# A linear-attention and token-mixer kernel: the attention output transposed by DMA instead of on TensorE, stores on SP, and one explicit table of steps

## The chip, the cores and the metric

The kernel runs on 1 core of a Trainium2 chip. The metric is the device time of one execution in microseconds. Engines are named as in the profile: PE is TensorE's matmul, PEld its weight load, DVE VectorE, ACT ScalarE, POOL GpSimd, SP SyncE. SPq and ACTq are the queues of SP and ACT when they issue DMAs. L12 is line 12 of the kernel before.

## The reference

Four batches, eight heads, 768 time steps, head size 48: a recurrent linear attention with a decay for each channel, followed by a token mixer.

```python
# attention; r, k, v, w: [4, 8, 768, 48]; u: [8, 48]
for t in range(S):
    cur = einsum('bhd,bhe->bhde', u[None] * kt, vt)
    y[:, :, t] = einsum('bhd,bhde->bhe', rt, state + cur)
    state = wt[:, :, :, None] * state + einsum('bhd,bhe->bhde', kt, vt)
# mixer; x = y as [4, 768, 384]; d_hyper = 64
wq, wk = x @ w_q, x @ w_k
W_tok = einsum('bsd,btd->bst', wq, wk) / sqrt(d_hyper)
out = maximum(einsum('bst,btd->bsd', W_tok, x), 0) @ w_out
```

## The kernel before

The 768 steps of a batch are cut into three tiles of 256 steps, so there are 12 tiles n = 3b + m. In a tile, partition p holds steps 2p and 2p + 1 (index j), and the partitions 0 to 63 and 64 to 127 are two chunks of 128 steps (index q). The state goes from chunk to chunk.

A tile runs through named steps, each a small Python function that issues its instructions:

- `load` (L146): w, k, r, v, 384 KB each, from SP, into buffers three deep.
- `log` (L153, ACT), `sums` (L158, PE): logarithm of the decay and its running sums, as matmuls with triangular matrices, into three PSUM tiles `cw`. `expk`, `expr`, `decay` (ACT) exponentiate them.
- `kdec` (L205, POOL) and `rdec` (L196, DVE): k and r times the decays, `KdS` and `RdS`. `uk1`, `uk2` (POOL), `red` (DVE), `vd` (POOL): the diagonal term, from `u*k*r`. `vcast` (ACT) writes v as bf16.
- `trR` (L214, PE), `evT` (L224, DVE): both decayed operands transposed into the PSUM tile `psT`, 16 transposes, and copied to `RKT`.
- `amat` (L230, PE), `mask` (L240, DVE): the products A inside a chunk, for each j, and their masking.
- `state`, `stadd` (PE), `stev` (L298, DVE): the new state in PSUM tile `Sn`, written to `SB`.
- `ymat` (L308), `yst` (L319), `yd` (L330), all PE: the output Y of the tile from A, from the state and from the diagonal.
- `yev` (L338): Y to bf16 as `X`. `xtr` (L348): X transposed on PE, six 128 x 128 blocks, into the PSUM tile `xt_ps`. `xev` (L358): copied to `XT`. `qkmat` (L365, PE) and `qkev` (L380): the products with w_k and w_q.

A batch then runs `tmat` (L386), `tev`, `mix` (L402), `mixev`, `fin` (L416), `finev` (L424), `store` (L431): since the mixer has no softmax, it is computed as a 64 x 384 matrix `Tps`, then `mps`, a ReLU and the product `fps` with w_out. A pair of output chunks goes out with two DMAs of 192 KB.

PSUM holds two large buffers (`psT`, A, `Sn`, Y take turns, L114) and four small ones (`cw`, `xt_ps`, `qk`, `Tps`, `mps`, `fps`, L117). An allocation waits until the use before it in that slot is done.

Seven tuples at L45 to L51 say which engine makes a copy: `EX` for X, `ET` for XT, `EQ` for qk, `EM` for the ReLU, `EF` for the output, 1 for ACT and 0 for DVE; `ES` says for each store whether ACT or SP issues it.

Every engine works in the order in which its instructions are issued. Before the change, each step has a due time (L501 to L665): a list of offsets for a first, a middle and a last tile, added to a start time for each tile, and the same for batches; the steps are sorted by due time (L681). `u` is loaded by `uload`, and `ucast` spreads it over the partitions with two f32 matmuls into `ups` and a DVE copy to `ubc`.

Of the kernel before, what the change touches and what calls it, by code (L numbers as in the profile page):

```python
# [12 lines left out]
BF16 = mybir.dt.bfloat16  # L13
# [12 lines left out]
def kernel(  # L26
# [12 lines left out]
    nc = tc.nc  # L39
# [5 lines left out]
    EX = (1, 1, 1, 1, 1, 1, 1, 1, 1, 1, 1, 0)  # L45
    ET = (1, 1, 1, 1, 0, 0, 0, 0, 0, 1, 1, 0)
    EQ = (1, 0, 1, 0, 0, 0, 1, 0, 1, 1, 1, 0)
    EM = (1, 1, 1, 0, 1, 0, 0, 1, 1, 0, 1, 1, 1, 1, 1, 1, 1, 1, 1, 0, 1, 1, 0, 1)
    EF = (0, 1, 0, 1, 1, 1, 1, 0, 0, 1, 1, 0, 1, 1, 1, 1, 1, 1, 0, 0, 0, 0, 0, 0)

    ES = (1, 0, 0, 1, 0, 1, 1, 1, 1, 1, 1, 0, 1, 1, 1, 1, 1, 1, 0, 1, 0, 1, 0, 0)  # L51
# [57 lines left out]
    sm = ctx.enter_context(tc.tile_pool(name="sm", bufs=3))  # L109
# [22 lines left out]
    plan = []  # L132

    def at(t, fn):
        plan.append((t, len(plan), fn))

    T = {}
# [6 lines left out]
    def load(n, nm, ap):  # L146
        b, m = divmod(n, NU)
        src = ap[b, :, ds(m * C2, C2)]
        t = ld.tile([C, H, D2], F32, name=nm + "G", tag=nm + "G")
        nc.sync.dma_start(out=t, in_=src.rearrange("h (p j) d -> p h (j d)", j=2))  # L150
        T[nm, n] = t
# [62 lines left out]
    def trR(n, j):  # L214
        T["trR", n, j] = True
        if ("psT", n) not in T:
            T["psT", n] = big([C, 2, 2, NP, C], BF16, "psT")
        o = T["psT", n][:, j]
        src = T[("Rd", "Kd")[j], n]
        for hp in range(NP):  # L220
            for jj in range(2):
                mm(o[:, :, hp, ds(jj * HC, HC)], src[:, jj, hp], ID128, trans=True)

    def evT(n):  # L224
        need(("trR", n, 0), ("trR", n, 1))
        RKT = bt.tile([C, 2, 2, NP, C], BF16, name="RKT", tag="RKT")
        nc.vector.tensor_copy(RKT, T["psT", n])  # L227
        T["RKT", n] = RKT

    def amat(n, js):  # L230
        RKT = T["RKT", n]
        A = big([C, 2, NP, C], F32, "A")
        for hp in range(NP):
            for q, hh in ((0, 0), (1, 1), (1, 0), (0, 1)):
                mm(A[ds(q * HC, HC), hh, hp],
                   RKT[ds(hh * 64, D), 1, q, hp, ds(js * HC, HC)],
                   RKT[ds(hh * 64, D), 0, q, hp], start=(hp == 0))
        T["A", n, js] = A
# [80 lines left out]
    def yst(n):  # L319
        T["yst", n] = True  # L320
        b, m = divmod(n, NU)
        for q in range(2):
            if 2 * m + q:
                SB = T["SB", b, 2 * m + q]
                for hp in range(NP):
                    mm(T["Y", n][:, q, ds(hp * D2, D2)], T["RKT", n][:, 0, q, hp],
                       SB[:, ds(hp * D2, D2)], start=False)
# [10 lines left out]
    def yev(n):  # L338
# [3 lines left out]
        if m == 0:  # L342
            T["X", b] = xpool.tile([C, NCH, DM], BF16, name="X", tag="X")
            T["XT", b] = xpool.tile([128, NK, S], BF16, name="XT", tag="XT")
# [3 lines left out]
    def xtr(n):  # L348
        need(("yev", n))
        b, m = divmod(n, NU)  # L350
        tp = mtile([128, NK, C2], BF16, "xt_ps")
        for cc in range(2):
            for dt in range(NK):
                mm(tp[:, dt, ds(cc * C, C)],
# [3 lines left out]
    def xev(n):  # L358
        T["xev", n] = True
        b, m = divmod(n, NU)  # L360
        copy(ET[n], T["XT", b][:, :, ds(m * C2, C2)], T["tp", n])
# [3 lines left out]
    def qkmat(n):  # L365
# [4 lines left out]
        for cc in range(2):  # L370
            for kt in range(NK):
                mm(qk[:, cc], XT[:, kt, ds((2 * m + cc) * C, C)], wk_sb[:, kt],
                   start=(cc == 0 and kt == 0))
        for kt in range(NK):
            for q in range(2):
                mm(qk[ds(q * DH, DH), 2:4].rearrange("p c h -> p (c h)"), T["wq"][:, kt],
                   XT[:, kt, ds((2 * m + q) * C, C)], start=False)
# [46 lines left out]
    def finev(b, c):  # L424
        T["finev", b, c] = True
        if c % 2 == 0:
# [66 lines left out]
    def wcast():  # L493
# [7 lines left out]
    steps = [  # L501
        (-3.67, log, ()),
        (-1.33, uk1, ()),
        (-0.45, sums, ()),
        (-0.42, expk, ()),
        (-0.25, expr, ()),
        (1.36, kdec, ()),
        (1.89, rdec, ()),
        (2.24, decay, ()),
        (3.56, uk2, ()),  # L510
        (5.7, trR, (1, )),
        (5.95, trR, (0, )),
        (5.99, vcast, ()),
        (6.48, red, ()),
        (6.51, vd, ()),
        (7.46, evT, ()),
        (8.59, amat, (0, )),
        (9.91, amat, (1, )),
        (10.1, mask, (0, )),
        (10.73, mask, (1, )),  # L520
        (11.87, state, ()),
        (11.9, stadd, (0, )),
        (12.36, stev, (0, )),
        (13.55, stadd, (1, )),
        (14.38, stev, (1, )),
        (15.25, ymat, ()),
        (15.48, yst, ()),
        (15.48, yd, ()),
        (15.51, yev, ()),
        (17.44, xtr, ()),  # L530
        (18.18, xev, ()),
        (20.45, qkmat, ()),
        (20.75, qkev, ()),
    ]
    first = [
        (-6.23, log, ()),
        (-6.05, sums, ()),
        (-2.68, expk, ()),
        (-0.31, decay, ()),
        (0.59, uk1, ()),  # L540
        (1.7, expr, ()),
        (3.15, kdec, ()),
        (5.93, trR, (1, )),
        (6.95, rdec, ()),
        (6.98, trR, (0, )),
        (7.64, evT, ()),
        (8.73, uk2, ()),
        (9.1, red, ()),
        (9.65, amat, (0, )),
        (9.93, amat, (1, )),  # L550
        (11.0, mask, (0, )),
        (12.22, mask, (1, )),
        (13.97, vcast, ()),
        (14.21, state, ()),
        (14.64, stadd, (0, )),
        (15.85, ymat, ()),
        (16.28, stev, (0, )),
        (16.31, stadd, (1, )),
        (16.31, yst, ()),
        (16.86, stev, (1, )),  # L560
        (16.87, vd, ()),
        (16.9, yd, ()),
        (17.07, yev, ()),
        (18.09, xtr, ()),
        (18.76, xev, ()),
        (20.43, qkmat, ()),
        (20.46, qkev, ()),
    ]
    last = [
        (-8.43, log, ()),  # L570
        (-0.36, sums, ()),
        (-0.33, expk, ()),
        (0.3, expr, ()),
        (0.33, rdec, ()),
        (0.47, decay, ()),
        (1.66, kdec, ()),
        (5.38, vcast, ()),
        (6.06, uk1, ()),
        (6.69, trR, (0, )),
        (7.03, trR, (1, )),  # L580
        (7.36, evT, ()),
        (7.73, uk2, ()),
        (9.43, amat, (0, )),
        (10.04, amat, (1, )),
        (11.58, state, ()),
        (13.51, red, ()),
        (14.13, mask, (0, )),
        (15.69, stadd, (0, )),
        (15.84, vd, ()),
        (15.86, mask, (1, )),  # L590
        (16.87, stev, (0, )),
        (17.84, ymat, ()),
        (17.87, yst, ()),
        (17.87, yd, ()),
        (21.51, stadd, (1, )),
        (29.8, yev, ()),
        (29.83, xtr, ()),
        (33.23, xev, ()),
        (33.26, qkmat, ()),
        (33.29, qkev, ()),  # L600
        (35.83, stev, (1, )),
    ]
    bsteps = [
        (-0.2, tmat, (0, )),
        (-0.17, tmat, (1, )),
        (0.03, tmat, (2, )),
        (0.67, tev, ()),
        (1.72, mix, (0, )),
        (1.75, mixev, (0, 0, )),
        (1.75, mixev, (0, 1, )),  # L610
        (3.02, mix, (1, )),
        (3.05, mixev, (1, 0, )),
        (3.05, mixev, (1, 1, )),
        (5.18, mix, (2, )),
        (5.5, mixev, (2, 0, )),
        (6.82, mixev, (2, 1, )),
        (7.09, fin, (0, )),
        (8.59, fin, (1, )),
        (8.71, fin, (2, )),
        (9.55, finev, (0, )),  # L620
        (9.58, finev, (1, )),
        (12.6, finev, (2, )),
        (13.11, store, (0, )),
        (13.4, fin, (3, )),
        (13.43, finev, (3, )),
        (15.19, store, (1, )),
        (15.4, fin, (4, )),
        (16.51, fin, (5, )),
        (16.54, finev, (4, )),
        (19.42, finev, (5, )),  # L630
        (19.68, store, (2, )),
    ]
    blast = [
        (12.66, tmat, (0, )),
        (12.96, tmat, (1, )),
        (13.44, tmat, (2, )),
        (13.55, tev, ()),
        (13.58, mix, (0, )),
        (14.09, mix, (1, )),
        (14.09, mix, (2, )),  # L640
        (14.12, mixev, (0, 0, )),
        (14.12, mixev, (0, 1, )),
        (14.12, mixev, (1, 0, )),
        (14.12, mixev, (2, 0, )),
        (14.63, mixev, (1, 1, )),
        (28.34, mixev, (2, 1, )),
        (28.37, fin, (0, )),
        (28.5, fin, (1, )),
        (29.14, fin, (2, )),
        (29.18, fin, (3, )),  # L650
        (29.23, finev, (0, )),
        (29.26, finev, (1, )),
        (29.73, store, (0, )),
        (29.74, fin, (4, )),
        (30.7, finev, (2, )),
        (31.09, finev, (3, )),
        (31.34, fin, (5, )),
        (33.84, store, (1, )),
        (34.01, finev, (4, )),
        (35.33, finev, (5, )),  # L660
        (35.36, store, (2, )),
    ]
    start = [0.42, 8.84, 16.14, 23.73, 31.34, 38.86, 46.52, 54.11, 61.53, 69.25, 76.58, 84.42]
    bstart = [40.55, 65.17, 85.94, 114.26]
# [48 lines left out]
```

## Time and profile before

| What | Value |
|---|---|
| Median of 3 runs | 123.33 us (122.84 to 123.74) |
| The profiled execution | 123.79 us |
| Its span, first to last instruction | 122.0 us |
| Mean granted PE clock | 0.971 |
| Data moved by DMA | 24.66 MB, 202 GB/s over the span |
| Chain that ended last, by engine | PE 68%, ACT 12%, DVE 6%, DMA 3%, POOL 3% |
| X transposes on PE | 72, 221 ns each, 6.1 us busy |
| Copies of them to XT | ACT 6 of 799 ns, DVE 6 of 551 ns |
| Output copies | ACT 13 of 484 ns, DVE 11 of 550 ns |
| State product in Y, 128 x 128 weights | 80, 208 ns each, 5.5 us busy |
| Loads, issue to landing | 3.4 to 6.6 us, median 4.9 |
| Last matmul ends, span ends | about 115.6 us, 122.0 us |

Busy time counts an instruction from start to modelled end. Matmuls overlap, so the distance between the starts of two groups is the time that a group takes up on PE. An idle time is put down to the instruction that released the engine.

### The profile page before, as it was taken

What the parts mean: (1) busy time and instruction counts of PE and PEld (TensorE: products, weight loads), DVE (VectorE), ACT (ScalarE), POOL (GpSimd) and SP (SyncE); (2) the same over time, 40 slices, a digit from 0 to 9 for tenths busy, and PEclk for the clock granted to TensorE, in tenths of its full rate; (3) what the DMA queues carried; (4) which work ended last, traced back from release to release, by engine and by line L of the source; (5) the groups of instructions that cost most, each with busy time, mean ns of one, the idle gap of its engine ahead of it and who ended that gap; (6) DMA issues with size and microseconds to landing.
All of it is one profiled execution on the core that took longest, in us unless ns stands there. A gap on an engine that the chain in (4) does not pass through costs nothing.

```text
span 122.0 us, 4284 instructions
## 1 busy us (share of the span) xinstructions
PE 100.1 (82%) x1822; PEld 64.6 (53%) x1822; DVE 91.8 (75%) x150; ACT 77.2 (63%) x146; POOL 84.7 (69%) x81
## 2 busy tenths in 40 slices
PE   0193938979898999999999899999999999966800
PEld 0133536557575766757657466576576666532400
DVE  6213596699798978999989998989989777253800
ACT  4236391689779868986685948976478966426000
POOL 8949899995999999599597995967839804000000
PEclk9999996799999999999999999999999999999985
DMA  3999999999999999899839999500552200573092
GB/s 77 322 325 325 323 320 341 292 232 318 236 256 273 288 300 263 230 266 247 245 75 329 348 269 252 149 0 0 134 129 52 82 5 0 129 181 85 24 283 83
DMA packets 54598, 24.66 MB, mean 202 GB/s; under 512 B 51121, under 2 KB 54578, under 8 KB 54578
## 3 DMA queue, kind: packets, MB, share of 16 engines
q1 hardware_dynamic: 52274, 21.24, 64.6%
q10 hardware_dynamic: 2304, 3.15, 9.1%
q8 instruction: 14, 0.23, 0.7%
q14 instruction: 6, 0.05, 0.1%
HBM read 19.66 MB, written 4.72 MB: 200 GB/s over the span
## 4 chain that ended last, share of the span: by engine, by line
PE 68%; ACT 12%; DVE 6%; DMA 3%; POOL 3%; issue 2%; ACTq 1%; SPq 1%; DVEq 0%
PE cw L66 12%; PE Y L66 11%; PE psT L66 10%; PE fps L66 10%; PE Sn L66 5%; PE A L66 5%; PE xt_ps L66 5%; PE qk L66 5%; PE Tps L66 4%; ACT X L130 3%; DMA u<-in_u_dram 3%; DVE AmB L244 3%; ACT XT L130 2%; PE mps L66 2%; POOL uk L250 1%
## 5 line engine op out<-in xcount | busy, mean ns | idle before, releaser
L244 DVE TENSOR_TENSOR AmB<-A,MASK 128x1024 bf16<-128x1024 f32 x24 | 28.8, 1219 | 1.3 <-PE A L66 1.2
L271 POOL TENSOR_TENSOR Vd<-V,diag 128x768 bf16<-128x768 bf16 x12 | 17.7, 1478 | 13.7 <-ACT X L130 3.4
L250 POOL TENSOR_TENSOR uk<-kG,ubc 128x768 f32<-128x768 f32 x12 | 21.8, 1816 | 1.7 <-DVE ubc L486 1.7
L178 ACT ACTIVATE em<-cw,bias 128x384 bf16<-128x384 f32 x24 | 13.0, 580 | 15.6 <-PE cw L66 15.6
L257 POOL TENSOR_TENSOR uk<-uk,rG 128x768 f32<-128x768 f32 x12 | 21.8, 1816 | 0.1
L207 POOL TENSOR_TENSOR KdS<-kG,em 128x768 bf16<-128x768 f32 x12 | 19.7, 1640 | 1.2 <-ACT em L178 1.2
L227 DVE COPY RKT<-psT 128x2048 bf16<-128x2048 bf16 x12 | 14.6, 1217 | 4.0 <-PE psT L66 4.0
L66 PEld LDWEIGHTS <-KdS 64*128 64x128 bf16 (+1 forms) x256 | 10.8, 99 | 9.1 <-POOL KdS L207 3.6
L200 DVE TENSOR_TENSOR RdS<-rG,cw 128x384 bf16<-128x384 f32 x24 | 12.2, 551 | 4.5 <-ACT cw L185 4.5
L66 PE MATMUL fps<-wout_sb,mixT 128*128 128x384 bf16 x72 | 14.6, 328 | 0.1
L302 DVE TENSOR_TENSOR SB<-Sn,pt 128x384 bf16<-128x384 f32 x20 | 11.0, 551 | 4.0 <-PE Sn L66 2.6
L66 PEld LDWEIGHTS <-RKT 48*64 48x64 bf16 (+1 forms) x464 | 10.3, 107 | 7.1 <-issue 4.5
L185 ACT ACTIVATE cw<-cw,bias 128x384 f32<-128x384 f32 x24 | 12.3, 553 | 0.2
L264 DVE TENSOR_REDUCE diag<-uk 128x16 f32<-128x768 f32 x12 | 11.3, 945 | 0.4 <-POOL uk L257 0.4
L155 ACT ACTIVATE logw<-wG 128x768 bf16<-128x768 f32 x12 | 10.2, 851 | 2.1 <-DMA wG<-in_w_dram 2.1
L66 PE MATMUL cw<-logw,BI 128*128 128x384 bf16 x36 | 11.5, 377 | 0.0
L66 PE MATMUL psT<-ID,KdS 128*128 128x128 bf16 x96 | 7.8, 227 | 4.0 <-DVE AmB L244 2.0
L66 PE MATMUL cw<-logw,BS 128*128 128x384 bf16 x36 | 11.0, 363 | 0.0
L66 PE MATMUL A<-RKT 48*64 48x128 bf16 x384 | 10.1, 226 | 0.8 <-ACT X L130 0.8
L130 ACT CAST X<-Y 128x768 bf16<-128x768 f32 x11 | 8.8, 800 | 2.9 <-PE Y L66 2.7
L211 ACT CAST V<-vG 128x768 bf16<-128x768 f32 x12 | 10.0, 841 | 0.0
L130 ACT COPY osb<-fps 128x384 f32<-128x384 f32 x13 | 6.1, 484 | 5.3 <-PE fps L66 2.1
(74 smaller groups left out, 165.1 us busy)
## 6 DMA issues: line engine op xcount, KB each, us to landing
wG<-in_w_dram SPq DMA_DIRECT2D x12, 384.0 KB, 5.5
kG<-in_k_dram SPq DMA_DIRECT2D x12, 384.0 KB, 5.1
rG<-in_r_dram SPq DMA_DIRECT2D x12, 384.0 KB, 4.8
vG<-in_v_dram SPq DMA_DIRECT2D x12, 384.0 KB, 4.9
out_dram<-osb ACTq DMA_DIRECT2D x16, 192.0 KB, 3.0
out_dram<-osb SPq DMA_DIRECT2D x8, 192.0 KB, 3.8
wout_f<-in_moe_w_out_dram SPq DMA_DIRECT2D x1, 576.0 KB, 4.7
wq_f<-in_moe_w_q_dram SPq DMA_DIRECT2D x1, 96.0 KB, 4.1
```

The lines of the kernel that those rows point to most:

```text
L66: nc.tensor.matmul(o, l, rr, start=start, stop=stop, skip_group_check=True, is_transpose=trans)
L130: (nc.scalar.copy if e else nc.vector.tensor_copy)(o, i)
L178: nc.scalar.activation(em[:, j], T["cw", n, 1 + j][:, 0:DM], ACT.Exp, bias=bias[2 + j], scale=-1.0)
L185: nc.scalar.activation(cw, cw, ACT.Exp, bias=bias[j], scale=1.0)
L200: nc.vector.tensor_tensor(pad(Rd)[:, j], jhd(T["r", n])[:, j], T["cw", n, j][:, 0:DM].rearrange("p (h d) -> p h d", d=D), ALU.mult)
L207: nc.gpsimd.tensor_tensor(pad(T["Kd", n]), jhd(T["k", n]), hd(T["em", n]), ALU.mult)
L227: nc.vector.tensor_copy(RKT, T["psT", n])
L244: nc.vector.tensor_tensor(T["AmB", n][:, js].rearrange("p q h t -> p h q t"), T["A", n, js], _rep(_rep(MASK[:, js], 1, NP), 1, 2), ALU.mult)
L250: nc.gpsimd.tensor_tensor(uk, T["k", n].rearrange("p h (j d) -> p h j d", j=2), _rep(ubc.rearrange("p (h d) -> p h d", d=D), 2, 2), ALU.mult)
L257: nc.gpsimd.tensor_tensor(uk, uk, T["r", n].rearrange("p h (j d) -> p h j d", j=2), ALU.mult)
L264: nc.vector.tensor_reduce(diag.rearrange("p j h -> p h j"), T["uk", n], axis=AX.X, op=ALU.add)
L271: nc.gpsimd.tensor_tensor(Vd, T["V2", n], _rep(T["diag", n], 3, D), ALU.mult)
```

## The change

The transpose of X goes to a DMA on SP for all tiles but the last (`DT`); for these, `xev` issues nothing. A second switch (`DR`), which would do the same for the decayed r, is 0 everywhere. The layouts of `XT`, `psT` and the transposed operands change with it, so that j stands ahead of the head pair and each transposed block is contiguous; `yst` therefore issues two matmuls of 64 weight columns where there was one of 128. The engines of the copies are chosen anew: 6 XT copies go from ACT and 5 from DVE, 5 qk copies and 10 output copies move from DVE to ACT, and one ReLU moves from ACT to DVE. Only three stores stay on ACT, all of the last batch. The state buffers go from three to five. The due times are replaced by one table that lists all steps in one order; loads are separate steps in it.

```diff
-    EX = (1, 1, 1, 1, 1, 1, 1, 1, 1, 1, 1, 0)
-    ET = (1, 1, 1, 1, 0, 0, 0, 0, 0, 1, 1, 0)
-    EQ = (1, 0, 1, 0, 0, 0, 1, 0, 1, 1, 1, 0)
-    EM = (1, 1, 1, 0, 1, 0, 0, 1, 1, 0, 1, 1, 1, 1, 1, 1, 1, 1, 1, 0, 1, 1, 0, 1)
-    EF = (0, 1, 0, 1, 1, 1, 1, 0, 0, 1, 1, 0, 1, 1, 1, 1, 1, 1, 0, 0, 0, 0, 0, 0)
-    ES = (1, 0, 0, 1, 0, 1, 1, 1, 1, 1, 1, 0, 1, 1, 1, 1, 1, 1, 0, 1, 0, 1, 0, 0)
+    EX = (1, 1, 1, 1, 1, 0, 1, 1, 1, 1, 1, 1)
+    ET = (0, 0, 0, 0, 0, 0, 0, 0, 0, 0, 0, 0)
+    EQ = (1, 1, 1, 1, 1, 1, 1, 1, 1, 1, 0, 1)
+    EM = (0, 1, 1, 1, 1, 1, 1, 1, 0, 1, 0, 1, 1, 1, 1, 0, 1, 1, 1, 0, 0, 1, 1, 0)
+    EF = (1, 1, 1, 1, 1, 1, 0, 1, 1, 1, 1, 1, 1, 1, 1, 1, 1, 1, 1, 1, 1, 1, 1, 1)
+    ES = (0, 0, 0, 0, 0, 0, 0, 0, 0, 0, 0, 0, 0, 0, 0, 0, 0, 0, 0, 1, 0, 1, 0, 1)
+    DT = (1, 1, 1, 1, 1, 1, 1, 1, 1, 1, 1, 0)
+    DR = (0, 0, 0, 0, 0, 0, 0, 0, 0, 0, 0, 0)
...
-    sm = ctx.enter_context(tc.tile_pool(name="sm", bufs=3))
+    sm = ctx.enter_context(tc.tile_pool(name="sm", bufs=5))
...
     def trR(n, a):
...
-                mm(o[:, :, hp, ds(jj * HC, HC)], src[:, jj, hp], ID128, trans=True)
+                mm(o[:, jj, hp], src[:, jj, hp], ID128, trans=True)
...
     def amat(n, js):
...
-                mm(A[ds(q * HC, HC), hh, hp],
-                   RKT[ds(hh * 64, D), 1, q, hp, ds(js * HC, HC)],
-                   RKT[ds(hh * 64, D), 0, q, hp], start=(hp == 0))
+                mm(A[ds(q * HC, HC), hh, hp].rearrange("p (j t) -> p j t", j=2),
+                   KT[ds(hh * 64, D), js, hp, ds(q * HC, HC)],
+                   RT[ds(hh * 64, D), :, hp, ds(q * HC, HC)], start=(hp == 0))
...
     def yst(n):
...
                 for hp in range(NP):
-                    mm(T["Y", n][:, q, ds(hp * D2, D2)], T["RKT", n][:, 0, q, hp],
-                       SB[:, ds(hp * D2, D2)], start=False)
+                    for j in range(2):
+                        mm(T["Y", n][ds(j * HC, HC), q, ds(hp * D2, D2)],
+                           T["RT", n][:, j, hp, ds(q * HC, HC)], SB[:, ds(hp * D2, D2)],
+                           start=False)
...
-            T["XT", b] = xpool.tile([128, NK, S], BF16, name="XT", tag="XT")
+            T["XT", b] = xpool.tile([128, NCH, NK, C], BF16, name="XT", tag="XT")
...
     def xtr(n):
         need(("yev", n))
         b, m = divmod(n, NU)
-        tp = mtile([128, NK, C2], BF16, "xt_ps")
+        if DT[n]:
+            nc.sync.dma_start_transpose(
+                out=T["XT", b][:, ds(2 * m, 2)].rearrange("p c k t -> p (c k) t"),
+                in_=T["X", b][:, ds(2 * m, 2)].rearrange("p c d -> p (c d)"))
+            return
+        tp = mtile([128, 2, NK, C], BF16, "xt_ps")
...
     def xev(n):
...
-        copy(ET[n], T["XT", b][:, :, ds(m * C2, C2)], T["tp", n])
+        if not DT[n]:
+            copy(ET[n], T["XT", b][:, ds(2 * m, 2)], T["tp", n])
...
-    steps = [
-        (-3.67, log, ()),
-        (-1.33, uk1, ()),
...
-    start = [0.42, 8.84, 16.14, 23.73, 31.34, 38.86, 46.52, 54.11, 61.53, 69.25, 76.58, 84.42]
...
+    order = (
...
+        (load, 2, "w"), (load, 2, "k"), (sums, 0), (load, 2, "r"), (load, 2, "v"),
+        (load, 3, "w"), (expk, 0), (wload,), (decay, 0), (kdec, 0), (ucast,), (expr, 0),
+        (vcast, 0), (rdec, 0), (trR, 0, 1), (uk1, 0), (log, 1), (load, 3, "v"), (state, 0),
...
+        (rdec, 10), (amat, 9, 0), (yev, 8), (mask, 9, 0), (qkmat, 7), (uk2, 11), (xtr, 8),
+        (amat, 9, 1), (qkev, 7), (fin, 1, 1), (red, 10), (trR, 10, 0), (finev, 1, 1),
+        (fin, 1, 3), (mask, 9, 1), (vd, 10), (store, 1, 0), (trR, 10, 1), (finev, 1, 3),
+        (fin, 1, 4), (store, 1, 1), (evT, 10), (xev, 8), (qkmat, 8), (finev, 1, 4), (state, 9),
...
+        (fin, 3, 2), (fin, 3, 3), (finev, 3, 2), (fin, 3, 4), (finev, 3, 3), (fin, 3, 5),
+        (finev, 3, 4), (store, 3, 1), (fin, 3, 0), (finev, 3, 5), (fin, 3, 1), (finev, 3, 0),
+        (store, 3, 2), (finev, 3, 1), (store, 3, 0),
+    )
     with tc.manual_schedule():
-        for _, _, fn in sorted(plan, key=lambda x: x[:2]):
-            fn()
+        for fn, *a in order:
+            fn(*a)
```

## Prediction

> **What bounds the kernel now.** I read the busy line of the page first, then the same in stretches, then the chain of waits, and last single rows for prices.
>
> ```profile
> PE 100.1 (82%) x1822; PEld 64.6 (53%) x1822; DVE 91.8 (75%) x150; ACT 77.2 (63%) x146; POOL 84.7 (69%) x81
> ```
> ```profile
> 11.30:25.00 13.70, 10.95 (x168) 7.51 (x168) 9.25 (x12) 7.17 (x13) 13.09 (x9) 0.88 1.12 314
> ...
> 40.00:55.00 15.00, 14.76 (x320) 9.91 (x320) 13.79 (x20) 12.90 (x24) 13.52 (x9) 1.00 1.02 271
> ...
> 85.00:100.00 15.00, 14.93 (x302) 9.67 (x299) 12.90 (x18) 10.42 (x23) 9.75 (x6) 1.00 0.31 82
> ```
> Columns: stretch, its length, busy us of PE, weight loads, DVE, ACT, POOL, granted clock, DMA share, GB/s. POOL is full from 11 to 25 us (13.09 of 13.70), PE from 40 to 100 us (14.8 to 14.9 of 15), with DVE close behind at 40 (13.79). DMA is full early and nearly idle late. So three stages: a head set by what POOL and PE get first, a middle where PE time is the span, a tail of single dependent steps.
>
> ```profile
> 1.85 3.55 DMA u<-in_u_dram
> ...
> 5.53 1.63 PE ups L66 x2
> ...
> 7.18 0.57 DVE ubc L486
> ...
> 7.83 1.81 POOL uk L250
> 9.64 1.60 POOL KdS L207
> ...
> 38.67 0.81 ACT X L130
> ...
> 39.53 0.51 PE xt_ps L66 x6
> ```
> In the chain (start, us, what) the head hangs on the small load of `u`, two f32 matmuls and the first `uk` on POOL; only then comes `KdS`, which the transposes on PE need. Further on, PE stands still while ACT writes X and then transposes it.
>
> **The change, part by part.** The profiled execution took 123.79 us for a span of 122.0; the median of the runs is 123.33, 0.46 less. I sum against 123.79 and take off 0.46 at the end.
>
> *1. Head: −2.3 us.* The table puts `sums 0` before `ucast` on PE and `kdec 0` before `uk1 0` on POOL. The log of tile 0 ends at 4.14 + 0.84 = 4.98, yet the first cw matmul starts at 7.08, behind the ups matmuls (5.53 to 7.15). The second `em` ends 2.30 after that start (8.80 + 0.58 = 9.38). With sums at 5.0, `kdec 0` can start at 7.3 instead of 9.64: −2.3. Its k load is issued at 1.24 and lands 3.4 to 6.6 later (median 4.9). From below: POOL is full here and only starts at 7.3 instead of 7.83, so −0.5. From above: before the end of `kdec 2` the new POOL order has 3 kdec, 4 uk and 1 vd, 3×1.64 + 4×1.82 + 1.48 = 13.7, so 21.0 against 23.37 + 1.64 = 25.0 now, −4.0. I take the middle one, which is the path to the first transposes.
>
> *2. PE work of the middle: −2.6 us.* 66 of 72 X transposes go. The price of one is the distance between starts, not its 221 ns, because matmuls overlap:
> ```profile
> 52.59 0.51 PE L66 MATMUL Y<-SB,RKT 128*128 128x96 bf16 x8
> 53.04 0.50 PE L66 MATMUL Y<-Vd,PERM 64*128 64x384 bf16 x4
> ...
> 57.12 0.36 PE L66 MATMUL qk<-XT,wq_sb 128*64 128x128 bf16 x6
> 57.41 0.62 PE L66 MATMUL psT<-ID,KdS 128*128 128x128 bf16 x8
> ...
> 100.73 0.51 PE L66 MATMUL xt_ps<-ID,X 128*128 128x128 bf16 x6
> 101.17 0.42 PE L66 MATMUL A<-RKT 48*64 48x128 bf16 x16
> ```
> Six X transposes take 101.17 − 100.73 = 0.44; 11 tiles give −4.8 (elsewhere the chain shows up to 0.46, and six starting at 54.78 are followed at 55.12, 0.34; so −3.7 to −5.1). Against it, `yst` now writes its 128 rows in two halves: 80 matmuls become 160, each with 64 weight columns. Eight old ones take 53.04 − 52.59 = 0.45. The nearest half-width pair, `qk<-XT,wq_sb`, takes 0.29 for six, 48 ns each with 128 moving columns; with 96 columns 36 to 48 ns. Sixteen cost 0.58 to 0.77, so +0.13 to +0.32 for a full tile, and 80/8 = 10 such: +1.3 to +3.2, I take +2.2. Net −2.6 (−0.5 to −3.8). `amat` and `trR` keep their counts and sizes and only swap strides: I cost that at nothing, as no count or size changes.
>
> [...]
>
> *3. Waits on X: −1.0 us.*
> ```profile
> PE xt_ps L66 <- ACT X L130: 1.6, 3, 0.5
> ...
> PE qk L66 <- DVE XT L130: 0.7, 1, 0.7
> ```
> Columns: total, times, longest. PE waited three times (0.53 each) for ACT's X before a transpose; the DMA takes that wait to SP. The `qk` wait belongs to the last tile, whose transpose stays on PE. Bounds 0 to −1.6: the next `amat` also needs X written, because the two large PSUM buffers turn over through Y, so part of the wait comes back one instruction later. I take −1.0.
>
> *4. Copies moved: nothing in the middle.* Eleven XT copies go (6 on ACT at 0.80, 5 on DVE at 0.55), 5 `qks` and 10 `osb` move from DVE to ACT, one `mixT` the other way, 13 of 16 stores leave ACT's queue (0.63 each). DVE: −2.75 − 2.1 + 0.55 − 5.5 = −9.8. ACT: −4.8 + 1.9 − 0.5 + 4.8 = +1.4, less 8.2 of issuing. PE hides all of it; if PE stopped being the limit, DVE's 82 us over 12 tiles, 6.8 per tile, would be the next floor, under the 7.9 that a tile takes now (first psT matmuls at 57.41 and, four tiles on, 89.13). Two more state buffers cost nothing that a row shows. Stores on SP stand behind loads that are long issued by then.
>
> *5. Tail: +0.45 us.* All six last `osb` copies go to ACT, with two store issues between them: 6×0.48 + 2×0.63 = 4.1 against 113.24 to 116.21 on DVE now, +1.2; the last two stores go out side by side on SP and ACT instead of one after the other, −0.6. The last X moves from DVE (0.96) to ACT (0.80), −0.15.
>
> *6. The transposes themselves: +1.0 us.* No row shows one. Each waits on SP for ACT (once DVE) to write X. Queued behind it are loads of later tiles, which in turn wait for POOL steps that come later still, so I cost the block on loads at nothing; its cover is the three-deep buffers, two tiles or 15 us. Who waits is `qkmat`, which stands in PE's queue: PE stops if the transpose has not landed. From the new order I add PE prices from the end of `yst n` to `qkmat n` and take off 0.8 for writing X. Tile 8: A 0.35, qk 0.57, A 0.35, three fps groups 1.77, psT 1.0 = 4.04, leaving 3.2. Tile 9: Sn 0.45, two state adds 0.2, three mps pairs 0.81, psT 1.0, Y 1.39, A 0.35 = 4.2, leaving 3.4. In the same way tile 6 has 3.8, tiles 5 and 10 4.5 (10 shares the wait of 9), tile 7 5.9; tiles 0 to 4 have a tile or more. With L from issue to landing, PE loses (L−3.2) + (L−3.4) + (L−3.8) + (L−4.5), each from zero up.
> ```profile
> out_dram<-osb ACTq DMA_DIRECT2D x16, 192.0 KB, 3.0
> out_dram<-osb SPq DMA_DIRECT2D x8, 192.0 KB, 3.8
> ```
> A transpose also moves 192 KB. Stores land after 2.7 at the least and 5.6 at the most, 384 KB loads after up to 6.6. I take SP's own median, L = 3.8: 0.6 + 0.4 = +1.0. Ends: 2.7 (nothing) and 6.6 (3.4 + 3.2 + 2.8 + 2.1 = +11.5). For tiles 5 to 10 the DMA engines are little used, which speaks for the lower half.
>
> [...]
>
> Sum: −2.3 − 2.6 − 1.0 + 0.45 + 1.0 = −4.45; 123.79 − 4.45 = 119.3, less 0.46: **118.9 us**.
>
> **The rivals.**
> *A. Transposes land late (slower).* The gains without term 6 are 5.45, so 4L − 14.9 = 5.45, L = 5.1 us is the break-even. At L = 6 PE loses 9.1: 127.0. At 6.6, 129.4; beyond, 4 us per us. For it: nothing in the trace prices a transposing DMA, and five tiles have under 4.6 us of cover. Against it: the late DMA is idle, and DVE's masks and copies between (2.4 and 1.2 per tile) may stretch the cover beyond PE's sums.
>
> *B. The PE time saved does not reach the end.* The two large PSUM buffers tie PE to DVE, which is 92% busy at 40 to 55 us. If terms 2 and 3 both fall away and term 1 is at its POOL end, −0.5 + 0.45 + 1.0 = +0.95: 124.3; with the head kept, 122.5; with half of terms 2 and 3, 120.7. For it: every engine's order is new and one misplaced step costs a wait. Against it: DVE sheds 9.8 us.
>
> *C. The change is not wholly made:* the last tile still goes through PE. That tile is on the tail, so the tail keeps its X, XT, qk steps, and I have given it no gain; no separate case.
>
> **Chances and range.** The forecast 0.46. B, 120.5 to 124.5, 0.20: half of it faster by over 1%, 0.07 within, 0.03 slower. A, 122 and up, 0.34, of which 0.02 within 1%. About 1% is what a measurement of this kernel can tell. Faster 0.46 + 0.10 = 0.56, same 0.09, slower 0.35. The best corner is −4.0 − 3.8 − 1.6 + 0.45 = −8.95, 114.4. The range runs from there to A at L = 6.6 to 6.8, some 130: that leaves out about 0.15 above and 0.05 below. The forecast's own range is 114.5 to 121.5.
>
> **What would show it.** Term 1: the first psT matmul near 9.0 instead of 11.29. Term 2: PE about 97 busy or less, and eleven xt_ps groups gone; `Y<-SB` groups of 16 taking 0.6 to 0.8. Term 3: no PE wait on X before 100 us. Term 5: ACT ending last, after the final stores' issue. Term 6 and A: issue-to-landing of XT<-X, and the idle time of PE or its weight loads before `qk`; under 4 us the forecast stands, above 5 it falls. B: PE idle in the middle with DVE or ACT as releaser. I am wrong outright if SP holds loads back behind a transpose, so that `logw`, `KdS` or `V` wait for DMA.

## The result, and the profile after

The changed kernel takes 131.17 us (median of 4 runs, 129.34 to 131.79) where the kernel before takes 123.53 in the same comparison: the ratio is 1.054, with a 95% interval of 1.041 to 1.068. The forecast was 118.9, the range ended at 130.0: the sign is wrong, and the range missed. The profiled execution, the slowest of the four, took 131.79 us for a span of 130.0 (before: 123.79 for 122.0); the two fastest runs have a mean of 130.1. Medians below are over all runs of a kernel, while ratios leave disturbed runs out, so the two can differ by about one per cent.

First the busy line of the changed kernel, then its stretches, with the columns of the prediction (stretch, length, busy us of PE, weight loads, DVE, ACT, POOL, granted clock, DMA share, GB/s):

```profile
PE 99.7 (77%) x1836; PEld 63.2 (49%) x1836; DVE 83.5 (64%) x131; ACT 80.1 (62%) x154; POOL 84.7 (65%) x81
```
```profile
25.00:40.00 15.00, 11.54 (x273) 8.40 (x272) 11.88 (x15) 10.84 (x20) 13.74 (x9) 0.89 1.09 253
40.00:55.00 15.00, 11.13 (x223) 7.39 (x216) 10.17 (x13) 10.53 (x19) 12.17 (x8) 0.89 1.20 250
55.00:70.00 15.00, 12.98 (x249) 8.15 (x250) 10.56 (x14) 10.86 (x23) 11.50 (x8) 0.89 1.16 274
70.00:85.00 15.00, 13.70 (x284) 8.79 (x281) 12.96 (x19) 11.28 (x23) 14.46 (x10) 1.00 1.10 241
```
Two stretches of the kernel before, which the prediction did not show, for comparison:

```profile
55.00:70.00 15.00, 14.45 (x279) 9.56 (x276) 14.33 (x22) 10.87 (x21) 12.79 (x9) 1.00 0.89 247
70.00:85.00 15.00, 14.72 (x289) 9.96 (x285) 13.95 (x21) 11.25 (x22) 11.82 (x8) 1.00 0.51 140
```
Before, the DMA share falls to 0.89 and 0.51 after 55 us, and PE is full. After, it stays at 1.1 to 1.2 until 85 us (a column of busy shares that goes above 1 counts some time more than once), PE stands at 11 to 14 of 15, and no other engine is full in its place but POOL from 70 to 85 us (14.46). DMA now ends idle time on four engines. These are the waits on DMA (total, times, longest); before, of the loads of w, k, r and v only w was waited for, 2.1 us once:

```profile
PEld L70 <- DMA XT<-X: 7.4, 6, 2.7
...
ACT logw L155 <- DMA wG<-in_w_dram: 6.6, 5, 2.3
PE qk L70 <- DMA XT<-X: 6.1, 6, 2.5
...
DVE RdS L200 <- DMA rG<-in_r_dram: 2.4, 1, 2.4
...
ACT V L211 <- DMA vG<-in_v_dram: 1.8, 2, 1.0
...
POOL uk L265 <- DMA kG<-in_k_dram: 1.2, 2, 1.0
```
Loads: 12.0 us; transposes at `qk`: 6.1 us. In the chain that ended last (start, us, what), DMA has 31% where it had 3%:

```profile
23.87 6.34 DMA wG<-in_w_dram
...
34.77 5.42 DMA wG<-in_w_dram
40.18 5.61 DMA XT<-X
45.84 0.64 PE qk L70 x12
...
55.23 6.32 DMA rG<-in_r_dram
...
71.08 3.96 DMA XT<-X
```
The queue of SP shows how the two meet (start, us of issue, what):

```profile
30.14 0.99 SPq L150 DMA_DIRECT2D wG<-in_w_dram  x1
31.23 2.20 SPq L369 DMA_TRANSPOSE XT<-X  x1
33.53 0.52 SPq L150 DMA_DIRECT2D kG<-in_k_dram  x1
34.14 2.59 SPq L150 DMA_DIRECT2D wG<-in_w_dram  x2
36.84 1.14 SPq L150 DMA_DIRECT2D rG<-in_r_dram  x1
38.07 2.02 SPq L150 DMA_DIRECT2D vG<-in_v_dram  x1
40.18 2.62 SPq L369 DMA_TRANSPOSE XT<-X  x1
```
One issue follows the other without a gap, and X of tile 0, whose transpose is the one at 31.23, had been written by 23.7. For tiles 0 to 4 alike, SP came to the transpose 7.5 to 8.4 us after X was written: it did not wait for X there, it was behind with the loads. A load's issue took 0.37 us in the median on SP where the queue had pauses (from 54 us on in the kernel before) and mostly 1.0 us or more between 5 and 50 us, in both kernels.

**Where the 8 us of span went.** PE's span is matmul work at full clock, plus what half a clock adds, plus idle time. The clock column gives the second: a stretch of 15 us at 0.89 has lost 1.65 us. The kernel before has one such stretch, the changed one four. Work: 99.7 − 4×1.65 = 93.1 against 100.1 − 1.65 = 98.5, so 5.4 us less. Half clock: 5.0 more. Idle: 30.3 against 21.9, 8.4 more, of which 25 to 85 us has 10.65 − 3.0 = 7.65, the head −1.6 and the stretch from 85 us on +2.4. The sum is +8.0. The work was saved as planned; waits, and the half-clock stretches that follow some of them (experiment 4), gave back more.

### The profile page after: what moved, and what is told of

Read it like the earlier page. It is cut to its first block, busy times and chain, and to the rows that moved or that the text cites. A ratio compares the mean times of both kernels' runs of the same rounds, so it can differ in the third digit from the quotient of the medians.

```text
span 130.0 us, 4343 instructions
## 1 busy us (share of the span) xinstructions
PE 99.7 (77%) x1836; PEld 63.2 (49%) x1836; DVE 83.5 (64%) x131; ACT 80.1 (62%) x154; POOL 84.7 (65%) x81
## 4 chain that ended last, share of the span: by engine, by line
PE 42%; DMA 31%; ACT 7%; DVE 5%; POOL 5%; issue 4%; ACTq 2%; DVEq 0%
DMA XT<-X 14%; DMA wG<-in_w_dram 12%; PE cw L70 11%; PE Y L70 7%; PE fps L70 6%; DMA rG<-in_r_dram 5%; PE psT L70 4%; PE qk L70 4%; PE A L70 3%; PE Sn L70 3%; POOL KdS L207 2%; PE Tps L70 2%; ACTq L457 2%; DVE RKT L242 2%; DVE RdS L200 1%
## 5 line engine op out<-in xcount | busy, mean ns | idle before, releaser
L134 ACT COPY osb<-fps 128x384 f32<-128x384 f32 x23 | 10.9, 478 | 10.1 <-PE fps L70 7.3
L70 PEld LDWEIGHTS <-RKT 48*64 48x64 bf16 (+1 forms) x544 | 11.0, 110 | 12.2 <-issue 9.8
L70 PE MATMUL cw<-logw,BI 128*128 128x384 bf16 x36 | 12.5, 409 | 5.2 <-ACT logw L155 5.2
L70 PEld LDWEIGHTS <-KdS 64*128 64x128 bf16 (+1 forms) x256 | 11.5, 101 | 6.8 <-issue 2.7
L70 PE MATMUL A<-RKT 48*64 48x128 bf16 x384 | 10.6, 232 | 3.8 <-DVE AmB L259 2.2
L70 PE MATMUL cw<-logw,BS 128*128 128x384 bf16 x36 | 12.1, 394 | 0.0
L70 PE MATMUL psT<-ID,RdS 128*128 128x128 bf16 x96 | 8.8, 242 | 1.6 <-DVE RdS L200 0.7
```

What stands on the lines that cost most here:

```text
L70: nc.tensor.matmul(o, l, rr, start=start, stop=stop, skip_group_check=True, is_transpose=trans)
L134: (nc.scalar.copy if e else nc.vector.tensor_copy)(o, i)
```

## The experiments

**1. Taking the DMA transposes out of the new table, whole and in halves.** `DT` is the tuple that chooses the path. Where a tile goes back to PE, its `xev` stands right behind its `xtr`, on DVE.

```diff
 e1:  DT = (0, 0, 0, 0, 0, 0, 0, 0, 0, 0, 0, 0)
 e2:  DT = (1, 1, 1, 1, 1, 0, 0, 0, 0, 0, 0, 0)
 e3:  DT = (0, 0, 0, 0, 0, 1, 1, 1, 1, 1, 1, 0)
-        (xtr, n), ... (xev, n), ... (qkmat, n)
+        (xtr, n), (xev, n), ... (qkmat, n)
```


> The changed kernel with every X transpose back on PE, each XT copy (DVE) right behind its transposes; table, copies and stores as changed. Theory W (PE waits at qkmat for transposes that land late) and theory Q (the transposes hold up SP's queue and the DMA engines, so loads come late) both expect the loss gone: 117 to 121 us, a ratio to before of 0.95 to 0.98. Theory T (the new table is slow by itself, because steps that need a load stand too early in ACT's and POOL's order) expects 126 or more.

> DMA transposes only for tiles 0 to 4, while loads run; tiles 5 to 11 on PE. Theory Q expects most of the loss here: 125 to 130. Theory W, with covers of a tile or more for these tiles, expects little: 119 to 122 if the landing takes no longer than 6 us. Theory T: as e1_all_pe, 126 or more.

> DMA transposes only for tiles 5 to 10; tiles 0 to 4 on PE. Theory W expects the loss here, by the landing of 3 to 5.5 us against covers of 3.2 to 4.5: 123 to 128. Theory Q, with the last loads issued near 75 us, expects 119 to 122. Theory T: 126 or more.

Measured: e1_all_pe 126.07 (124.83 to 127.96), ratio 1.011 (1.002 to 1.020); e2_dma_early 131.76, ratio 1.061 (1.051 to 1.071); e3_dma_late 127.14 (124.94 to 127.92). The five early transposes alone cost as much as all eleven (ratio 1.061 against 1.054), while the runs with the six late ones lie within the spread of e1_all_pe. Without any, the new table is still not faster than before, though both theories that blame the transposes expected 117 to 121 us.

**2. Transposes and copies that nobody reads.** On top of e1_all_pe, SP moves every X once more into a spare buffer `XD`, as a DMA transpose or as a plain copy, either where the change has its transpose or one tile later, when X has long been written.

```diff
     def xtr(n):
+        XD = xpool.tile([128, 2 * NK, C], BF16, name="XD", tag="XD")
+        nc.sync.dma_start_transpose(out=XD, in_=X of tile n)      # e1d
+        nc.sync.dma_start(out=XD, in_=X of tile n)                # e1copy
+        ... of tile n - 1 instead                                 # e1dl, e1cl
         tp = mtile([128, 2, NK, C], BF16, "xt_ps")
```


> As e1_all_pe, and the 11 DMA transposes are issued as well, at their place on SP, into a buffer that nobody reads. Theory Q expects the cost of their traffic and of the blocked queue without any wait at qkmat: 124 to 130, well above e1_all_pe. Theory W expects e1_all_pe within 1.5 us. The load wait rows (logw, V, RdS, uk released by DMA) should be near the 12 us of the changed kernel by Q, near e1_all_pe's by W.

> As e1d_unread, but the 11 unread DMAs are plain copies of the same 192 KB, at the same place on SP. Q1 expects e1d_unread's time, 130 to 134: the same wait in the same place. Q2 expects a third of its loss, in proportion to DMA time (0.7 us for a copy at the loads' rate against 2.0): 127 to 129, with DMA share and load waits near e1_all_pe's.

> As e1d_unread (all X transposes on TensorE, eleven unread DMA transposes on SP), but at tile n the DMA transposes X of tile n-1, which has been written for some 8 us: SP never stands waiting for X, while bytes and transposes are the same. Theory Q1 (the loss is SP's queue: loads stand behind a transpose that waits for its X): 126-128.5, near e1_all_pe's 126.1. Theory Q2 (the loss is the time that the transposes take of the 16 DMA engines): 131-133, as e1d_unread's 132.8.

> As e1copy_unread (unread plain copies of X, the same bytes as the transposes), but each one tile late, when its X has long been written, so that SP never waits for X. If hold and DMA time add up: e1_all_pe's 126.1 and, of the 3.6 us that the unheld transposes cost, the share of a copy's DMA time in a transpose's (some 0.7 of 1.95 us), 1.3 us: 127.4 (126.5-128.5). If holding were all: 126. If any extra DMA on SP costs the same whatever its kind: 129.7 as e1dl_unread_late.

| On top of e1_all_pe: 126.07, two fastest 125.0 | at once | one tile later |
|---|---|---|
| DMA transposes | 132.81 (129.04 to 135.03), two fastest 129.8 | 129.68 (128.45 to 130.96), two fastest 128.7 |
| plain copies | 130.60 (128.21 to 132.15), two fastest 128.7 | 128.59 (126.85 to 130.45), two fastest 127.3 |

The first number is the median of all runs, the last the mean of the two fastest. No matmul and no copy waits for `XD`, and yet the two fastest rise by 2.3 to 4.8 us; the two fastest of the change are 5.1 above e1_all_pe's. So most of the loss needs no wait at `qkmat`. Why "at once" costs about 1 us more than "one tile later" is not shown: in e1d_unread, too, SP reached the transposes of tiles 0 to 4 6.5 to 8.2 us after X was written, so it was not held by an unwritten X there.

Two other things grew with the added DMAs, and the experiments do not separate them from late loads. In the tail, ACT's first store issue of the last batch takes 2.4 to 2.6 us in all four kernels where e1_all_pe has 0.72; in the profiles of e1d_unread, e1dl_unread_late and e1copy_unread the last X is written 1.6 to 2.3 us later than in e1_all_pe, and the rest of their 3.4 to 4.2 us, 1.9 to 2.0, is this tail. And e1d_unread and e1copy_unread have some 13.7 us at half clock, as the change, where e1_all_pe has 6.8.

What a transpose takes of the engines is in the queue line (packets, MB, share of 16 engines' span) and the issue line, for e1_all_pe, e1d_unread and e1copy_unread in turn:

```profile
q1 hardware_dynamic: 54146, 23.80, 71.7%
```
```profile
q1 hardware_dynamic: 62946, 25.96, 86.2%
...
XD<-X SPq DMA_TRANSPOSE x11, 5.4
```
```profile
q1 hardware_dynamic: 55730, 25.96, 75.2%
...
XD<-X SPq DMA_DIRECT2D x11, 192.0 KB, 4.3
```
With the second queue (1.4%, 1.6%, 1.6%) the engines are taken for 73.1% of 122.8 = 89.8 us, 87.8% of 127.0 = 111.5 and 76.8% of 126.2 = 96.9. By these differences a transpose takes 21.7/11 = 1.97 us of all sixteen engines in 800 packets, a copy of the same bytes 7.1/11 = 0.65 us in 144. For this shape a transpose thus took three times the engine time of a copy.

The waits for loads stand at 5.4 us in e1_all_pe, 15.2 in e1d_unread and 17.2 in e1dl_unread_late, by the same rows of the waits as above. Their sum is no price, though: it is 5.9 in e1copy_unread, 8.8 in e1cl_copy_late and 9.8 in e2_dma_early.

**3. Another queue, another order.** In e4_act_queue ACT issues the transposes. In ashift_late_order SP does, one tile later, and `qkmat` follows later too.

```diff
 e4_act_queue
-            nc.sync.dma_start_transpose(
+            nc.scalar.dma_start_transpose(
 ashift_late_order
-        (yev, n), ... (xtr, n), ... (yev, n + 1)
+        (yev, n), ... (xtr, n), (yev, n + 1)          for n = 0 to 4
-        (qkmat, 0), (qkev, 0), ... (yev, 2)
+        (yev, 2), ... (qkmat, 0), (qkev, 0), (yev, 3)  and 1, 3, 4 alike
```


> The changed kernel, its 11 transposes issued from ACT's queue, right behind the write of X, instead of from SP's. Theory Q1 (SP is held up: loads and stores stand behind a transpose that waits for X and takes 2.0 us to issue) expects the loads on time and 124 to 127. Theory Q2 (the transposes' own traffic, some 2 us of all 16 DMA engines each, crowds out the loads on whatever queue) expects 129 to 135, more than the changed kernel since ACT now spends 11 x 2 us issuing.

> The changed kernel with the DMA transposes of tiles 0 to 4 set one tile later in the table (just ahead of the next tile's yev) and qkmat and qkev of tiles 0, 1, 3 and 4 set up to a tile later, so that SP meets an X that is written already and TensorE an XT that has landed. Same transposes, same bytes. Theory Q1 (hold and waits are the loss): 126-128. Theory Q2 (the DMA time of the transposes, which starves the loads whatever the order): 129.5-131.5, as after. By the square so far (hold 3.1 of the 6.7 us between e1d and e1, bytes 3.6): 127.5-129.

Measured: e4_act_queue 134.59 (131.92 to 135.68); ashift_late_order 132.95 (131.17 to 137.09), ratio 1.066 (1.060 to 1.073). e4_act_queue is slower than the change itself, and ashift_late_order is not faster (the intervals overlap). In ashift_late_order ACT waits for w only 2.6 us instead of 6.6, and PE in return at `qk` (the waits, then the longest of them in PE's timeline, with the idle time and its releaser at the end):

```profile
PE qk L70 <- DMA XT<-X: 8.1, 3, 5.4
...
ACT logw L155 <- DMA wG<-in_w_dram: 2.6, 2, 2.2
```
```profile
51.88 0.50 PE L70 MATMUL qk<-wk_sb,XT 128*128 128x64 bf16 x6 [5.38 <-DMA XT<-X]
```
In this table the order that serves the loads first makes the transposes late, and the other way round: of the orders tried, none gained by moving a transfer in front of another. In e4_act_queue loads are waited for 21.4 us, though no transpose stands on their queue.

**4. Half-clock spells.** In the changed kernel PE's granted clock was 0.50 for 3.4 us four times, each time after 3.4 us in which PE had been idle for 33 to 54% of the time. One such pair:

```profile
30.60:34.00 3.40, 1.57 (x38) 1.03 (x34) 2.78 (x3) 3.40 (x6) 3.40 (x3) 1.00 0.97 250
34.00:37.40 3.40, 3.10 (x55) 2.46 (x54) 2.83 (x5) 2.40 (x6) 2.32 (x3) 0.50 1.25 173
```
Three kernels put unread matmuls into such gaps: w1_filled_gaps into five of the changed kernel, e1fill_gaps into three of e1_all_pe, bfill_head into the first of the kernel before.

```diff
+    def fill(n):
+        t = mtile([C, 2, C], F32, "idle")
+        for _ in range(n):
+            mm(t, ID128, MASK)
 w1, e1fill:  (stadd, 0, 1), (fill, 10) ... (amat, 0, 1), (fill, 5) ... (fill, 14), (state, 1)
 w1 only:     18 such matmuls ahead of qkmat 1, 8 ahead of qkmat 2
 bfill:       at(10.5, lambda: fill(18))
```


> The changed kernel with matmuls that nobody reads put where TensorE sat idle in it: 15 beside the first tile's amat steps, 14 ahead of state 1, 18 ahead of qkmat 1, 8 ahead of qkmat 2 (0.107 us each at full clock, 5.9 us in all, placed in idle stretches of 1.2 + 0.7, 1.6, 2.5 and 1.0 us). Everything else as it was. Theory H (after a stretch of some 3.4 us in which TensorE is half idle, its clock is halved for the next 3.4 us; four such spells cost the changed kernel 6.6 us of matmul time against 1.7 before): two or three spells fewer, the time falls by 2 to 5 us, to 126-129. Theory T (the spells fall where TensorE would have waited for loads and DMA anyway): spells fewer, time 130-132. If the added matmuls only get in the way: 132-134.

> e1_all_pe with 15 unread matmuls beside the first tile's amat steps and 14 ahead of state 1 (0.107 us each), where TensorE sat idle 2.6 and 1.6 us and a half-clock spell followed each time (3.4 us of matmul time lost in all, before 1.7). Theory H (spells cost what they take): both gone, 123-125 against e1_all_pe's 126.1. Theory T (the first 40 us go at the pace of the loads and POOL, as two trials at the head showed): within 0.7 us of 126.1.

> The kernel of before with 18 unread matmuls (1.9 us at full clock) in the idle 2.0 us of TensorE behind the first two amat steps (16.2 to 18.2 us). Theory H: the one half-clock spell of 19.2 to 22.6 us, which costs 1.7 us of matmul time, is gone, and the time falls by 0.5 to 1.7 us, to 122-123. Theory P (the first 25 us go at the pace of POOL and of the loads, as when the first transposes came earlier and nothing was gained): within 0.4 us of before.

Measured: w1_filled_gaps 129.89 (128.41 to 130.98), ratio 1.044 (1.035 to 1.052), with two spells instead of four; e1fill_gaps 125.76, ratio 1.014 (1.009 to 1.019), one instead of two; bfill_head 123.68, ratio 0.999 (0.995 to 1.003), its one spell only moved, from 19.2 to 25.5 us. The spells are real, but taking away one before 40 us gained nothing in e1fill_gaps; that something slower sets the pace there fits, and was not shown. Later ones may cost part of the 1.3 us that w1_filled_gaps gained; its interval overlaps that of the change, and one of its two spells is a new one at 75 us, so theory H is not shown in size.

**5. The head.** e7_head_alone is the kernel before with the two moves that term 1 rests on, and nothing else. e1p_less_pool takes POOL work away.

```diff
 e7_head_alone
-        (0.59, uk1, ()),
+        (3.2, uk1, ()),
-    at(-99.0, ucast)
+    at(3.0, ucast)
 e1p_less_pool
     def uk1(n):
         uk = hw.tile([C, H, 2, D], F32, name="uk", tag="uk")
+        if n < 6:
+            T["uk", n] = uk
+            return
```


> The kernel before with nothing but the order of its head changed: ucast behind the first running sums on PE, kdec 0 ahead of uk1 0 on POOL. My term 1 expects -2.3 us: 121.0 to 121.5. Theory P expects POOL's end of that term, -0.5: 122.5 to 123.5, with the first psT matmul near 9.2 all the same.

> e1_all_pe without uk1 for tiles 0 to 5 (uk2 multiplies k by r; u is left out of the diagonal term of these tiles), which takes 6 x 1.82 us from POOL. Theory P (POOL sets the pace of the first tiles, so the earlier start of the head is lost to it) expects X of tile 3 and of tile 4 earlier by 2 to 5 us and a total of 121 to 124. If PE's or the loads' pace set it, X of tile 3 comes within 1 us of e1_all_pe's 45.9 and the total within 1.5 us.

Measured: e7_head_alone 123.81 (10 runs, 123.20 to 124.22), ratio 1.0005 (0.998 to 1.003). Its first transposes do start 2.1 us early, but tile 1's `KdS` is only 0.4 us earlier than before, and tile 3's is later (first psT, then that `KdS`; before: 11.29 and 31.48):

```profile
9.19 1.03 PE L66 MATMUL psT<-ID,KdS 128*128 128x128 bf16 x8 [0.17 <-POOL KdS L207]
```
```profile
31.81 1.65 POOL L207 TENSOR_TENSOR KdS<-kG,em 128x768 bf16<-128x768 f32 x1
```
Where the gain went shows in DVE's timeline. `red` of tile 0 stands ahead of the first masks in DVE's order and waits 2.15 us for POOL's `uk2`, which the move has left no earlier. The masks start at 16.87 us (before: 16.90), and the second transposes on PE wait for them 3.9 us instead of 2.0:

```profile
15.08 0.95 DVE L264 TENSOR_REDUCE diag<-uk 128x16 f32<-128x768 f32 x1 [2.15 <-POOL uk L257]
...
16.87 2.35 DVE L244 TENSOR_TENSOR AmB<-A,MASK 128x1024 bf16<-128x1024 f32 x2
```
```profile
18.14 1.01 PE L66 MATMUL psT<-ID,KdS 128*128 128x128 bf16 x8 [3.94 <-DVE AmB L244]
```
So in the kernel before it was POOL's unchanged sum of work, met through `red`, that ate the head's gain. The new table orders these steps differently (the first mask of tile 0 stands ahead of `red 0`), and there POOL's work is not the limit: e1p_less_pool has 10 us less of it, its X of tile 3 starts at 45.53 us against 45.91, and it takes 125.08 us, ratio 1.011 (1.005 to 1.017), the same as e1_all_pe. What sets the pace of the head in the new table stays open; the DMA share of 1.02 over the first 25 us of e1_all_pe fits the loads, and was not shown by itself.

**6. The same idea where the DMA engines are free.** The kernel before with DMA transposes for a few late tiles, every split and, but for `qkmat` and `qkev` of these tiles, every order as it was.

```diff
+    DT = (0, 0, 0, 0, 0, 0, 1, 1, 0, 1, 1, 0)      # blate;   blate2: tiles 7, 9, 10
             xtr, xev, qkmat and the layout of XT as in the change
+            dt += 4.0 if DT[n] and fn in (qkmat, qkev) else 0.0      # blate2: 6.0
             at(start[n] + dt, lambda n=n, fn=fn, a=a: fn(n, *a))
```


> The kernel of before, order and splits kept, with the X transposes of tiles 6, 7, 9 and 10 alone made by DMA on SP, whose loads are all issued by then, and the qkmat and qkev steps of these four tiles 4 us later in the plan; XT laid out as in the changed kernel. Takes 24 transposes of 66.5 ns (1.6 us) off TensorE where it is busy over 98 % (55 to 100 us), and four copies off ACT and DVE. Theory L (the idea is sound and pays where the DMA engines are half idle and nothing stands behind on SP): 1.0 to 1.6 us faster, 122 to 122.5. Rival: another engine sets the pace there (DVE is busy 14.3 of 15 us in 55 to 70): within 0.5 us of before. If the transposes still land late: slower.

> As blate_dma_6_7_9_10 without tile 6, and with qkmat and qkev of tiles 7, 9 and 10 moved by 6 us of the plan instead of 4. In that run tile 6's X lay some 6 us behind the last load on SP, tile 7's transpose behind tile 6's, TensorE waited 2.4 us at qkmat 6 and a half-clock spell of 1.7 us followed, against 2.0 us of matmul time saved. Here 18 transposes of 66.5 ns (1.2 us) leave TensorE, and nothing stands ahead on SP. Theory L (pays where the queue and the DMA engines are free): 122.0 to 122.8, 0.5 to 1.2 us faster than before. Rival (TensorE's work is not what the end waits for, or a wait comes elsewhere): 123.2 or more.

blate_dma_6_7_9_10 took 126.02 us, ratio 1.012 (1.005 to 1.019): a miss. Tile 6's X was written by 69.6 us, but its transpose stood behind a load and a store until 75.15, and tile 7's behind it. In SP's queue and then in PE's timeline:

```profile
73.43 0.37 SPq L151 DMA_DIRECT2D vG<-in_v_dram  x1
73.85 1.20 SPq L441 DMA_DIRECT2D out_dram<-osb  x1
75.15 3.22 SPq L353 DMA_TRANSPOSE XT<-X  x2
```
```profile
79.32 0.35 PE L67 MATMUL qk<-wk_sb,XT 128*128 128x64 bf16 x6 [2.42 <-DMA XT<-X]
```
Without tile 6, blate2_dma_7_9_10 took **121.74 us** (6 runs, 121.34 to 122.04), ratio 0.985 (0.982 to 0.988): faster than both kernels. Its transposes land after 3.2 to 4.4 us, PE has 98.4 us busy in a span of 119.8, and from 70 to 85 us PE is as full as before (columns as above):

```profile
70.00:85.00 15.00, 14.72 (x287) 9.49 (x279) 14.07 (x21) 11.84 (x23) 12.97 (x9) 1.00 0.69 146
```
The gain, 2.0 us, is more than the matmul time of three groups of transposes, 3 × 0.44 = 1.3 us by the row in the prediction; three copies fewer on ACT and DVE and 0.5 us less idle time on PE are in the rest, which I did not take apart. The later place of `qkmat` and `qkev` was not tried without the DMAs, so a part of the gain may be the order's.

**7. Why the table alone is not faster.**

```diff
 e1ld_loads_by_tile:  the 48 loads in the order w, k, r, v of tile 0, then of tile 1, ...
                      (log, n) behind (sums, n - 1), (vcast, 11) behind (vcast, 10)
 e1xev_later_act
-    ET = (0, 0, 0, 0, 0, 0, 0, 0, 0, 0, 0, 0)
+    ET = (1, 1, 1, 1, 0, 0, 0, 0, 0, 1, 1, 0)
-        (xtr, n), (xev, n), ...
+        (xtr, n), ... up to nine steps ... (xev, n)
```


> e1_all_pe with the 48 loads put through the same places of the table tile by tile (w, k, r, v of one tile, then of the next, as before), where the table draws the w of later tiles ahead of the r, k and v of earlier ones; log n stands right behind sums n-1, vcast 11 behind vcast 10. If the order of the loads is what the table loses by (ACT waits 3.6 us for w, DVE and POOL 1.8 us for r and k in e1_all_pe): 123.5-124.8. If not: 125.3-127.

> e1_all_pe with each xev up to nine steps later than its xtr instead of right behind it, and on the engines that the kernel before used (ACT for tiles 0 to 3, 9 and 10). If the 2.5 us were e1_all_pe's own (DVE stands 4.9 us at these copies waiting for TensorE, with mask and RdS work queued behind): 123.5-124.8. If the table's: 125.3-127.

e1ld_loads_by_tile took 131.99 us, ratio 1.063 (1.054 to 1.071); e1xev_later_act 127.87, ratio 1.033 (1.025 to 1.041). Neither repaired the table; both made it worse. In the first, ACT's waits for w grow from 3.6 to 11.1 us:

```profile
ACT logw L155 <- DMA wG<-in_w_dram: 11.1, 5, 3.9
```
So loads that come late cost some 6 us in this table with no DMA transpose at all, which is about what the DMA transposes cost it (`log` and one `vcast` moved too, so the size is not the loads' alone). Why e1_all_pe is 1.1% slower than before stays open; its two 0.89 stretches and 5.0 us of PE idle time from 25 to 55 us (before: one, and 2.2) show where, not why.

## Why the prediction was wrong

**Term 6, the transposes: this step failed.** "I cost the block on loads at nothing; its cover is the three-deep buffers, two tiles or 15 us." The buffers gave no such cover: the sixteen engines were busy from 11 to 55 us already, at a share of 1.12 and 1.02 in the very stretch rows that the prediction quotes, and SP's queue had no pause of over 0.6 us until 52.7 us. I read that figure as a property of the head and asked only whether the late DMA was idle. Eleven transposes add about 21.7 us of engine time, and six of them fall before the last load. In the changed kernel SP's queue has no pause of over 0.6 us until 74 us, and loads are waited for 12.0 us, against 2.1 before and 5.4 in e1_all_pe. The condition that I wrote down as "wrong outright", `logw`, `KdS` or `V` waiting for DMA, came true in `logw` (6.6 us; 3.6 in e1_all_pe) and `V` (1.8; 0.7); `RdS`, which I had not named, has 2.4. Experiments 1 and 2 show that this work on SP and the engines is the loss: e2_dma_early has the whole of it, and unread transposes cost nearly as much as read ones (4.8 and 5.1 us by the two fastest runs). How much of it passes through late loads, through half-clock stretches and through the long store issue in the tail was not separated.

In the same term, "tiles 0 to 4 have a tile or more" did not hold. "Each waits on SP for ACT" did not hold for these tiles either: tile 0's X was written at 23.7 us, and its transpose was issued at 31.23, behind loads that were late themselves. PE waited 0.3, 2.5 and 1.0 us for tiles 0 to 2, 3.8 us where I had none; for tiles 5 to 10 it waited 2.3 us (0.3, 1.7, 0.2) where I had 1.0. The prediction took the DMA engines for little used from tile 5 on; the rows between those it showed have 0.89 and 0.51 in the kernel before. L was 5.2 us in the median and 5.9 at most, inside my ends of 2.7 and 6.6, but by the early tiles, which my formula left out. For the late tiles alone its median was 2.8 (e3_dma_late), under my 3.8.

**Rival A** had the sign, with L = 5.2 against a break-even of 5.1, but not the mechanism: it lets `qkmat` wait and nobody else. By its formula L = 5.2 gives about no change. A rival that was missing is "DMA becomes the bound".

**Term 1, head.** The first psT came at 9.22 as said (9.0), and yet the 2.3 us did not reach the end: alone it is worth nothing (e7_head_alone, ratio 1.0005), because DVE's `red` waits for the same POOL work in front of the first masks (experiment 5). I had the lower bound, −0.5, and chose the middle as "the path to the first transposes". A path to a first step is not a path to the end.

**Term 2, PE work.** The transposes' −4.8 fits: PE's busy time at full clock fell by 5.4. The split of `yst`, which I had at +2.2, was mis-sized; sixteen half-width matmuls take as long as eight full ones:

```profile
29.00 0.53 PE L70 MATMUL Y<-SB,RKT 128*64 128x96 bf16 x16
29.46 0.42 PE L70 MATMUL A<-RKT 48*64 48x128 bf16 x16
```
That is 0.46 us from start to start against 0.45 before. The nearest row that I used, `qk` with 48 ns for one, was not near enough. The error went in the change's favour.

**Rival B** had the fate of this work: nothing of it reached the end, since PE was no longer the limit. That holds for the reason of DMA, not of DVE, which fell from 91.8 to 83.5 busy as I had counted.

**Term 3** cannot be told apart: PE's waits on X are gone and others stand there. **Term 4** held as far as it goes: DVE −8.3 (I had −9.8), ACT +2.9 (+1.4). **Term 5**, the tail, was mis-sized: from the start of the last X to the end it is 17.3 us against 15.5, +1.8 where I had +0.45. One of ACT's store issues took 2.45 us there instead of 0.63, with two output copies behind it; in e1_all_pe it took 0.72 and the tail 15.4. The long issue (2.4 to 2.8 us) is in every profile of the new table with DMA transposes or added copies on SP, and not in e4_act_queue, where ACT issues them; but e1xev_later_act, which has none at all, shows it too, so its cause is open.

**The table as a whole** I took for harmless beyond these terms. e1_all_pe has terms 1, 2's `yst`, 4 and 5 and no DMA transpose: −2.3 + 2.2 + 0.45 = +0.35 by my numbers, −1.85 with `yst` at nothing. It measured 1.1% slower, +1.4 us. That miss of 1 to 3 us is open; the other 5 us, from there to the change, are the transposes.

## What to carry to other kernels

Before work is moved to DMA, read the DMA share in the stretch where the new transfers will run, not on the average: where it was at 1 already (1.01 to 1.12 from 11 to 55 us in the kernel before), they cost time in each queue and each place in the order that was tried here. Price a transposing DMA by engine time and packets (here 1.97 us of all sixteen engines in 800 packets), not by bytes: a copy of the same 192 KB took 0.65 us in 144. Three transposes moved where the queue was empty (shares of 0.51 and 0.31 in the kernel before) gained 1.5%; five moved where it was full lost 4.9% (e2_dma_early's ratio 1.061 against e1_all_pe's 1.011).

## What the hardware did that I had not expected

- A DMA transpose of 192 KB inside SBUF took about 1.97 us of all sixteen DMA engines, a plain copy 0.65; 800 packets against 144 (experiment 2). Its issue on SP took 1.2 us at the least and 2.6 at the most in the changed kernel.
- PE's clock halved for 3.4 us at a time, with starts that lie whole periods of 3.41 us apart: in the changed kernel at 16.9, 34.0, 47.6 and 64.7 us, that is after 5, 4 and 5 periods (in e1ld_loads_by_tile once for three of them, 36.3 to 46.6 us). The stretches before them had PE busy 46, 46, 52 and 67%; one with 58% (23.7 to 27.1 us) was not followed by a spell, so the busy share alone does not decide.
- The clock column has 1.00 in the first stretches of a profile, but the rows do not bear it out: in the kernel before, eight transposes of `KdS` take 1.03 us at 11.29 us, as in a spell (1.03 at 35.84 us in the changed kernel), and 0.61 us at 18.17. In the changed kernel, too, the first eight take 1.03 us, at 9.22.
- Two matmuls with 64 weight columns each took no longer than one with 128: 0.46 us for sixteen of `yst` against 0.45 for eight.
